# K1's scores by column halves and the WO result in halves, with a new order, in a chained attention kernel on one core

## The chip, the cores and the metric

The kernel runs on one core of a Trainium2 chip. The metric is the device time of one execution in microseconds, as the median of several runs.

## The reference

A pre-norm block: attention with a recurrent memory, then a normed MLP. Sizes: 2048 tokens of width 512, 32 heads of 128, a memory of 8 rows, segments of 32 tokens, so 64 segments one after the other; MLP width 1792.

```python
for s in range(n_seg):
    xs = x[:, s * seg_len:(s + 1) * seg_len, :].copy()
    h = jnp.concatenate([mem, xs], axis=1)
    q = jnp.einsum('btd,dhe->bhte', h, Wq)
...
    scores = jnp.einsum('bhqe,bhke->bhqk', q, k) * scale
    scores = jnp.where(mask[None, None], scores, -1000000000.0)
    p = _softmax(scores, axis=-1)
    o = jnp.einsum('bhqk,bhke->bhqe', p, v)
    o = jnp.einsum('bhte,hed->btd', o, Wo)
    mem = o[:, :M, :].copy()
    outs.append(o[:, M:, :])
```

The eight memory rows of a segment's result feed the next segment's projections. That is the recurrence: projections, scores, softmax, value product, WO, memory rows, next segment. With h = x + attention(layernorm(x)), the output is h + MLP(layernorm(layernorm(h))).

## The kernel before, in words

The kernel records every operation with what it reads and writes (class `Sched`), then orders each engine's queue itself. TensorE's order is written out by hand in `ORDERS` (L37), one list for each class of segment (number modulo 4). The other engines' operations are placed by a list scheduler (`schedule`) that takes their due times from `PLAN` (L43) and, for some, their engine from `HOME` (L100); operations without a due time go by rank into gaps. `wire` then sets the semaphore waits. Each queue runs in order. `PHASE` (L25) gives the place in TensorE's instruction stream, modulo 256, at which a segment should begin, which filler weight loads (L870) are put in to reach.

A segment packs 24 new tokens and the 8 memory rows as a stationary operand `hT` of 128x32 per chunk of 128 input features (four chunks); the last eight tokens of every segment (`hB`) are projected four segments at a time, a block ahead, as filler work. The heads are in two halves, r = 0 and 1. In a segment:

- Q0, Q1, K0, K1 (L872, and L605 where the loaded weights are kept): projections of one half of the heads, four units of four matmuls of 128x512 each, one unit per chunk, into a PSUM bank.
- Copies of these on ACT (`kq`, L890, L891), then 32x32 turns on DVE into `QT` and `KALL` (L913), and a copy of the memory queries into `ZC` on POOL (L927).
- SC0, SC1 (L1037): the scores of the memory queries, onto a bank prefilled with the mask (L1012). Then on DVE the negated maximum `nmc` (L1045), on ACT two exponentials with sums (L1054), on DVE a reciprocal (L1059) and a product by it and by `even` (L1062, `PC`, a scalar-tensor-tensor, STT below) for each of two column groups, and a turn (`PTC`, L1064).
- V0, V1: projections of the values (L872); copies to `VS`.
- PV0, PV1 (L1075, L1080): the value products of the memory queries, both into banks 0 and 1, copied to `OT` (ACT, L890). PVA (L1143): the same for the ordinary queries of the segment before.
- WO (L1171): eight units of 128x256 into one bank; a turn on DVE (`TT`, L1183) and adds of its two halves: `hT` (L1177, the memory rows of the next segment) and `opT` (L1177, the finished rows).
- SA (L1105): the scores of the ordinary queries, with a softmax of its own on DVE, ACT and POOL (`nma`, `SA`, `sma`, `rsa`, `PA`, `PTA`, `BD`: L1115 to L1132).
- F0, F1: the filler, eight units per segment of the block's last eight tokens: K for class 0, Q for class 1, V for class 2, and WO for class 3 (L1210), with their copies and turns (`KB`, `QTB`, `VSB`, `TTB`).

Layernorms and their statistics (`stt`, `agg`, L806, L807; `st2`, L1249) also run on DVE, and the MLP follows after the last segment.

Of the kernel before, what the change touches and what calls it, by code (L numbers as in the profile page):

```python
# [1689 lines left out]
```

## Time and profile before

| | |
|---|---|
| median of 3 runs | 807.39 us (806.82 to 807.42) |
| profiled execution, span | 805.9 us |
| mean granted TensorE clock | 0.993 |
| busy: PE, DVE, ACT, POOL | 775.0, 621.0, 527.1, 349.6 us |

The profiled execution's own time is the span; the page gives no other for it, and it lies 1.5 us below the median of the runs. On a timeline line the columns are the start, the duration, the engine, the line of the kernel, the operation, its output and inputs, the partitions x elements, how many were merged, and in brackets the engine's idle time before it with what ended it. PE rows are matmuls, PEld their weight loads. In the groups the last columns are busy time, mean ns of one and idle time before.

### The profile page before, as it was taken

To read this page: it belongs to the slowest core of one execution; us is meant where nothing else is said; L and a number is where in the kernel's file an instruction comes from. 1 tells how busy PE (TensorE), PEld (TensorE's weight loads), DVE (VectorE), ACT (ScalarE), POOL (GpSimd) and SP (SyncE) were. 2 spreads that over 40 slices of the span, in tenths; PEclk is the share of its full clock that TensorE was granted. 3 is DMA by queue.
4 is the path that set the end of the run, shared out by engine and by line. 5 is a ranking of instruction groups with operands and counts; after the bars stand their busy time and mean duration, and the time that the engine had idled before them with its cause. 6 is when DMAs were issued, how large, how long until landed. Compare 5 with 4: busy or idle time off the path is not lost.

```text
span 805.9 us, 43594 instructions
## 1 busy us (share of the span) xinstructions
PE 775.0 (96%) x19308; PEld 422.5 (52%) x18891; DVE 621.0 (77%) x2008; ACT 527.1 (65%) x1522; POOL 349.6 (43%) x886
## 2 busy tenths in 40 slices
PE   3788999999999999999999999999999999999998
PEld 1345555555555555555555555555555555544443
DVE  3268897989898989898989898989899887824211
ACT  2446777777777777777777777777676766643342
POOL 5023334545454545454545454545463535267200
PEclk9989999999999999999999999999999999999999
DMA  9950010111101010101010202020212131264200
GB/s 340 392 185 16 4 29 11 30 31 29 31 21 39 17 43 17 43 11 50 9 45 10 50 11 50 11 49 3 51 29 62 40 86 29 88 170 130 69 27 26
DMA packets 65449, 48.03 MB, mean 60 GB/s; under 512 B 29028, under 2 KB 61676, under 8 KB 65260
## 3 DMA queue, kind: packets, MB, share of 16 engines
q1 hardware_dynamic: 64928, 44.98, 19.0%
q8 instruction: 150, 2.46, 1.2%
q14 instruction: 39, 0.32, 0.1%
q10 hardware_dynamic: 332, 0.27, 0.1%
HBM read 31.08 MB, written 8.13 MB: 49 GB/s over the span
## 4 chain that ended last, share of the span: by engine, by line
PE 91%; DVE 3%; DMA 2%; SPq 2%; ACT 1%; issue 1%; POOL 0%
PE ps L872 43%; PE ps L1171 16%; PE ps L605 6%; PE quad L1579 6%; PE ps L1572 5%; PE ps L1210 4%; PE quad L1075 3%; DMA WQ<-in_A_Wq_dram 2%; SPq L775 2%; PE ps L1105 2%; PE quad L1037 2%; PE ps L1365 2%; PE quad L1143 1%; PE quad L1080 1%; DVE PC L1062 1%; ACT kq L890 1%
## 5 line engine op out<-in xcount | busy, mean ns | idle before, releaser
L872 PE MATMUL ps<-WQ,hT 128*32 128x512 bf16 x2048 | 157.4, 382 | 3.4 <-DVE hT L1177 3.3
L1171 PE MATMUL ps<-WO,OT 128*32 128x256 bf16 x4224 | 140.8, 275 | 1.0 <-ACT OT L890 1.0
L872 PE MATMUL ps<-WV,hT 128*32 128x512 bf16 x1780 | 138.7, 379 | 0.0
L891 ACT ACTIVATE kq<-ps 128x512 bf16<-128x512 f32 x146 | 87.2, 597 | 63.7 <-PE ps L872 63.4
L1126 POOL TENSOR_TENSOR PA<-SA,rsa 128x256 bf16<-128x256 f32 x64 | 39.9, 624 | 183.0 <-DVE rsa L1119 170.6
L890 ACT CAST kq<-ps 128x512 bf16<-128x512 f32 x160 | 93.4, 584 | 38.2 <-PE ps L872 38.2
L1171 PEld LDWEIGHTS ps<-WO,OT 128*32 128x32 bf16 x4224 | 96.2, 97 | 26.5 <-ACT OT L890 12.3
L1132 POOL COPY BD<-PTA 32x192 bf16<-32x192 bf16 x256 | 95.5, 373 | 16.6 <-DVE PTA L1128 0.8
L1062 DVE SCALAR_TENSOR_TENSOR PC<-EC,rsc,even 128x128 bf16<-128x128 f32 x256 | 94.5, 370 | 6.7
L872 PE MATMUL ps<-WK,hT 128*32 128x512 bf16 x1292 | 92.5, 379 | 0.0
L872 PEld LDWEIGHTS ps<-WQ,hT 128*32 128x32 bf16 x2048 | 57.0, 96 | 57.9 <-issue 18.7
L913 DVE STREAM_TRANSPOSE KALL<-kq 128x256 f32<-128x256 f32 x160 | 70.5, 440 | 20.8 <-ACT kq L890 18.6
L1054 ACT ACTIVATE EC<-quad,nmc 128x64 f32<-128x64 f32 x252 | 77.1, 311 | 5.9 <-DVE nmc L1045 0.2
L605 PE MATMUL ps<-WK,hT 128*32 128x512 bf16 x756 | 74.6, 379 | 0.0
L890 ACT CAST VS<-ps 128x512 bf16<-128x512 f32 x126 | 73.7, 585 | 0.7
L890 ACT CAST OT<-quad 128x128 bf16<-128x128 f32 (+1 forms) x205 | 66.3, 363 | 7.5 <-PE quad L1080 5.7
L913 DVE STREAM_TRANSPOSE QT<-kq 128x256 f32<-128x256 f32 x128 | 57.0, 445 | 15.5 <-ACT kq L891 14.1
L872 PEld LDWEIGHTS ps<-WV,hT 128*32 128x32 bf16 x1780 | 50.5, 96 | 34.2 <-issue 1.0
L1575 ACT ACTIVATE WQ<-ps,b1t 128x512 bf16<-128x512 f32 x42 | 28.9, 688 | 52.0 <-PE ps L1572 52.0
L872 PEld LDWEIGHTS ps<-WK,hT 128*32 128x32 bf16 x1292 | 36.4, 97 | 46.1 <-issue 20.1
L1117 ACT ACTIVATE SA<-SA 128x256 f32<-128x256 f32 x64 | 26.7, 417 | 49.4 <-DVE SA L1116 45.0
L1223 POOL TENSOR_TENSOR opT<-TTB,TTS 32x64 bf16<-32x64 f32 x128 | 40.3, 315 | 31.7 <-DVE opT L1177 22.5
(160 smaller groups left out, 1477.9 us busy)
## 6 DMA issues: line engine op xcount, KB each, us to landing
WV<-in_A_Wv_dram SPq DMA_DIRECT2D x4, 1024.0 KB, 10.3
WK<-in_A_Wk_dram SPq DMA_DIRECT2D x4, 1024.0 KB, 18.0
WQ<-in_A_Wq_dram SPq DMA_DIRECT2D x4, 1024.0 KB, 19.0
WO<-in_A_Wo_dram SPq DMA_DIRECT2D x16, 256.0 KB, 7.6
v_last<-VSB SPq DMA_DIRECT2D x60, 64.0 KB, 3.1
VBD<-v_last SPq DMA_DIRECT2D x60, 64.0 KB, 2.8
h_mid<-xr SPq DMA_DIRECT2D x16, 128.0 KB, 1.8
WQ<-h_mid SPq DMA_DIRECT2D x4, 512.0 KB, 4.4
```

What stands on the lines that cost most here:

```text
L605: return e.add_instruction(mybir.InstMatmult(name="I-%d" % (4000000 + _kept[0]), engine=mybir.EngineType.PE, start_tensor_calc=start, stop ...
L872: ins = e.matmul(o, l, m, start=(k == 0), stop=(k == DC - 1), tile_position=(0, 32 * j), skip_group_check=True)
L890: return {"act": (lambda e: e.copy(out, src), t_act(n, ps_)), "dve": (lambda e: e.tensor_copy(out, src), 0.155 + 1.0e-3 * n * fast)}
L891: return {"act": (lambda e: e.mul(out, src, scale_), t_act(n, ps_)), "dve": (lambda e: e.tensor_scalar(out, src, scale_, None, ALU.mult), ...
L913: S.op("dve", lambda e: e.transpose(out, src), reads=[("kq", i)], writes=[key], dur=t_dve(256) + 0.02)
L1054: return e.activation(EC[:, r, sl, :], o[:, sl, :], ACTF.Exp, bias=nmc[:, r, sl:sl + 1], accum_out=smc[:, r, sl:sl + 1])
L1062: S.op("dve", lambda e, sl=sl, xc=xc: e.scalar_tensor_tensor(PC[:, r, :, :, sl], xc, rsc[:, r, sl:sl + 1], ev, ALU.mult, ALU.mult), reads= ...
L1132: S.narrow(S.op("pool", lambda e, j=j, rows=rows: e.tensor_copy(BD[rows, par, :, j, :, :], PTA[rows, :, 0:NA, :]), reads=["PTA"], writes=[ ...
L1171: ins = e.matmul(ps[bank][32 * j:32 * j + 32, 0:256], lhs(slot(h)), wo_cols(h, b), start=(k == 0), stop=(k == 15), tile_position=(0, 32 * ...
L1223: return e.tensor_tensor(o[32 * q:32 * q + 32, c:c + 2], x, y, ALU.add)
L1572: ins = e.matmul(ps[bank][:, 0:SBT], W1[:, cc, fc * P:(fc + 1) * P], hnT_of(k)[:, cc, :], start=(cc == 0), stop=(cc == DC - 1))
L1579: S.op("pe", lambda e: e.matmul(quad[:, t, :], gT_of(k, fc)[:, t * P:(t + 1) * P], W2[:, fc, :], start=(fc == 0), stop=(fc == FC - 1)), re ...
```

## The change

- K1 is projected by column halves (`half_passes`): eight units of four 128x256 matmuls in the order `KSEQ`, the first half into bank 2 and the second into bank 0. Each half has its own copy (`kql`, `kq`) and turn (`KAl`, `KA`).
- SC1 becomes SC1 and SC2, eight matmuls each, in banks 2 and 3, each with a prefill of its own (64 columns) and a maximum of its own (`nmc`, `nmd`). SC0 goes to bank 1.
- For the first half of the heads (`NRM` = 1) the two reciprocals and two STT become one reciprocal of two columns, a small product with `even` (`rse`) and one 128x256 product into `PC`. The second half keeps its two STT.
- WO's bank is turned in two halves (`TT2`), and the memory rows are added per half: chunks 0 and 1 first (`hTl`), then 2 and 3 (`hTm`). A projection unit waits only for its chunk's half.
- New `ORDERS`, `PLAN`, `HOME` and `PHASE`; a planned operation is never placed ahead of one planned before it on its engine.
- `PVM` and `P3` are off, so the paths they guard aren't built. All of PSUM becomes one tensor, `banks`, and `b1n` shares the place of `oN`.

```diff
-PHASE = (0, 64, 128, 192)
+PHASE = (11, 75, 139, 203)
+TT2, SPL, KCOL, PVM, NRM, P3 = True, True, True, False, 1, False
+KSEQ = ((0, 0), (1, 0), (1, 1), (0, 1), (0, 2), (0, 3), (1, 3), (1, 2))
...
-BANK = dict(K0=7, K1=6, Q0=6, Q1=5, V0=7, V1=5, F0=4, F1=6, FB=4, SA=5, WO=7, SC0=3, SC1=2)
+BANK = dict(K0=7, K1=2, KX=0, Q0=6, Q1=5, V0=7, V1=5, F0=4, F1=6, FB=4, SA=5, WO=7, SC0=1, SC1=2, SC2=3, PV0=5)
...
-                i = bisect.bisect_right(ST, t)
+                i = max(bisect.bisect_right(ST, t), placed[eng] + 1 if fixed else 0)
...
+        def half_passes(lhs, reads, slot, W, key, r, banks):
+            for n, (h, cc) in enumerate(KSEQ):
...
+                        w = W[:, cc, r * 2048:(r + 1) * 2048].rearrange("p (a y b e) -> p y a b e", a=4, y=2, b=2)[:, h, :, :, 32 * j:32 * j + 32]
+                        o, l, m = ps[banks[h]][32 * j:32 * j + 32, 0:256], lhs(cc), w
...
+            if r == 1 and SPL and s > 0:
+                for h, (a, b) in enumerate((("kql", "KAl"), ("kq", "KA"))):
...
+                    S.either(copy2(half, v, 256), reads=[("ps", bh)], writes=[(a, r)])
...
+                if not whole:
+                    S.op("dve", lambda e, sl=sl, o=o: e.tensor_reduce(nmc[:, r, sl:sl + 1], o[:, sl, :], AX.X, ALU.max, negate=True), reads=[bkey], writes=[("nmd" if sl else "nmc", r)], dur=0.22)
...
+            if NRM >> r & 1:
+                S.op("dve", lambda e: e.reciprocal(rsc[:, r, :], smc[:, r, :]), reads=[("sa", r), ("smc", r)], writes=[("rsc", r)], dur=0.16)
...
+                f = lambda e: e.tensor_tensor(PC[r][:].rearrange("p k t a -> p k a t"), bass.AP(x.tensor, x.offset, [list(x.ap[0]), [0, 2], [64, 2], [1, 64]]),
+                                              bass.AP(w.tensor, w.offset, [list(w.ap[0]), [2, 2], [1, 2], [0, 64]]), ALU.mult)
...
+            for h, k_ in enumerate(("TTl", "TT") if TT2 else ("TT",)):
+                w, c = (2, slice(2 * h, 2 * h + 2)) if TT2 else (4, slice(0, 4))
...
+                    S.op("dve", lambda e, c=c: [halves_add(tt, q2, hT[64 * q2:64 * q2 + 64, sl, c, NA:SEG], slice(NA, SEG), c)(e) for q2 in range(2)][1],
+                         reads=[(k_, par)], writes=[(HK[h], sl)], dur=0.36 if TT2 else 0.4)
```

What this makes of the queues is seen at three places. First TensorE in a class 0 segment, from the last unit of K1 to the value products. Before (WK,hT is K1, WV the values, WK,hB the filler, KALL,ZC the scores, PTC,VS is PV0):

```order
L872 MATMUL ps<-WK,hT 32x512 x12
L1037 MATMUL quad<-KALL,ZC 32x64 x16
L872 MATMUL ps<-WV,hT 32x512 x4
L605 MATMUL ps<-WV,hT 32x512 x4
L872 MATMUL ps<-WV,hT 32x512 x12
L872 MATMUL ps<-WK,hB 32x512 x4
L1037 MATMUL quad<-KALL,ZC 32x64 x16
L872 MATMUL ps<-WV,hT 32x512 x4
L872 MATMUL ps<-WK,hB 32x512 x4
L872 MATMUL ps<-WV,hT 32x512 x8
L872 MATMUL ps<-WK,hB 32x512 x4
L1075 MATMUL quad<-PTC,VS 128x2x16 x8
```

The same stretch of TensorE's queue in the changed kernel (L631 keeps the loaded weights):

```order
L925 MATMUL banks<-WK,hT 32x256 x4
L1099 MATMUL banks<-KALL,ZC 32x64 x16
L905 MATMUL banks<-WV,hT 32x512 x4
...
L631 MATMUL banks<-WV,hT 32x512 x4
L1099 MATMUL banks<-KALL,ZC 32x64 x8
L905 MATMUL banks<-WV,hT 32x512 x4
L631 MATMUL banks<-WV,hT 32x512 x4
L1099 MATMUL banks<-KALL,ZC 32x64 x8
L905 MATMUL banks<-WV,hT 32x512 x4
L631 MATMUL banks<-WV,hT 32x512 x4
L905 MATMUL banks<-WK,hB 32x512 x12
L1208 MATMUL banks<-PTC,VS 128x2x16 x8
```

Six units stood between SC0 and SC1 and five between SC1 and PV0; now four stand before the first part, two between the parts and five behind the second.

Second, DVE in the same stretch, from the second turn of QT to the second PTC. Before:

```order
L913 STREAM_TRANSPOSE QT<-kq 128x256
L1045 TENSOR_REDUCE nmc<-quad 128x2
L913 STREAM_TRANSPOSE KALL<-kq 128x256
L1059 RECIPROCAL rsc<-smc 128x1
L1062 SCALAR_TENSOR_TENSOR PC<-EC,rsc,even 128x128
L1059 RECIPROCAL rsc<-smc 128x1
L1045 TENSOR_REDUCE nmc<-quad 128x2
L1062 SCALAR_TENSOR_TENSOR PC<-EC,rsc,even 128x128
L1064 STREAM_TRANSPOSE PTC<-PC 128x128
L1059 RECIPROCAL rsc<-smc 128x1
L1062 SCALAR_TENSOR_TENSOR PC<-EC,rsc,even 128x128
```

DVE's queue at that place in the changed kernel (rse and the 128x2x2x64 product are the first half's, the two maxima 128x1 the second's):

```order
L965 STREAM_TRANSPOSE QT<-kq 128x256
L1110 TENSOR_REDUCE nmc<-banks 128x2
L979 STREAM_TRANSPOSE KALL<-kq 128x4x32 x2
L1116 TENSOR_REDUCE nmc<-banks 128x1
L1137 RECIPROCAL rsc<-smc 128x2
L1139 TENSOR_TENSOR rse<-rsc,even 128x4
L1142 TENSOR_TENSOR PC<-EC,rse 128x2x2x64
L1116 TENSOR_REDUCE nmc<-banks 128x1
L1148 RECIPROCAL rsc<-smc 128x1
L1153 STREAM_TRANSPOSE PTC<-PC 128x128
L1151 SCALAR_TENSOR_TENSOR PC<-EC,rsc,even 128x128
```

The second part's maximum and the first reciprocal of the second half now stand ahead of the first PTC.

Third, DVE at the end of a class 2 segment, from the second PTC to the scores of SA. In the changed kernel (stt and st are statistics of the layernorms, agg their aggregates):

```order
L1153 STREAM_TRANSPOSE PTC<-PC 128x128
L942 CAST OT<-banks 128x16x24
L1317 TENSOR_TENSOR opT<-TT 64x4x24 x2
L1073 COPY banks<-maskCF 128x64
L836 BN_STATS stt<-xr 128x6
L837 BN_AGGR agg<-stt 128x2
L1392 BN_STATS st<-xr 128x6
L1325 STREAM_TRANSPOSE TT<-banks 128x128
L1396 BN_AGGR agg<-st 128x2
L1317 TENSOR_TENSOR hT<-TT 64x2x8 x2
L1325 STREAM_TRANSPOSE TT<-banks 128x128
L1255 TENSOR_REDUCE nma<-banks 128x8
```

Before, two OT casts, a 128-column mask copy, stt and agg stood between PTC and the single TT, and st stood elsewhere. In class 0 the two opT adds stand behind rsa and ahead of the first QT in the changed kernel:

```order
L1357 STREAM_TRANSPOSE TTB<-banks 128x512
L1258 TENSOR_REDUCE sma<-SA 128x8
L1259 RECIPROCAL rsa<-sma 128x8
L1317 TENSOR_TENSOR opT<-TT 64x4x24 x2
L965 STREAM_TRANSPOSE QT<-kq 128x256
```

Before, that place had TTB, sma, rsa and QT alone, and the opT adds stood behind the second PTC.

More of the change, by code (lines that the diff above doesn't have):

```diff
@@ L1027, in sc_mm @@
             reg = 2 + bk % 2
+            heads = range(4) if part is None else range(2 * part, 2 * part + 2)
             def f(e):
-                for i in range(4):
+                for i in heads:
                     for j in range(4):
@@ new lines, in pair, with late_rows @@
+        def pair(s, r):
+            return 0 if r == 0 or not P3 else BANK["PV1"] if s > 0 else 2
+        def late_rows(s, r):
+            bk, sg = s // 4, s % 4
+            b0 = pair(s, r)
+            src = bass.AP(banks[:].tensor, banks[:].offset + 512 * b0 + MEM, [list(banks[:].ap[0]), [512, 2], [16, 8], [1, 8]])
+            ot = OTB[:, bk % 2, :, 8 * sg:8 * sg + 8].rearrange("p (t r k) q -> p r t k q", t=2, r=2)[:, r]
+            S.either(copy2(ot, src, 128), reads=[("ps", b0), ("ps", b0 + 1)], writes=[("OTB" if r else "OTC", bk % 2, sg)])
@@ L1081, in f @@
+                    ins = e.matmul(o, VBD[rows, bk % 2, sg, r, :], PTC[r][rows, :, 32:64, :].rearrange("p b q a -> p b a q"),
                                    start=False, stop=True, tile_position=(64 * t, 0), skip_group_check=True)
                 return ins
-            S.op("pe", f, reads=[("VS", s % 3, r), ("PTC", r)] + [("VBD", bk % 2, j) for j in range(4)], writes=CQ, dur=0.205, mode=MH, ni=20)
-            src = bass.AP(quad[:].tensor, quad[:].offset + 128 * r, [list(quad[:].ap[0]), [512, 2], [16, 8], [1, MEM]])
+            S.op("pe", f, reads=[("VS", s % 3, r), ("PTC", r)] + [("VBD", bk % 2, j) for j in range(4)], writes=both, dur=0.205, mode=MH, ni=20)
```

399 lines of the change are left out of this document (264 added, 135 removed), and 6 rows, old and new, of the table ORDERS.

## Prediction

> **What bounds the kernel now.** The page first, for its span; then the timeline of one segment on all engines; then the busy time by segment; then the groups by form, for prices.
>
> ```profile
> span 805.9 us, 43594 instructions
> ```
>
> A PE that the views call busy can hide waits, since the ends of matmuls are modelled; their starts tell more. Here is the segment that begins at 411.86 (class 0, by number modulo 4); the last row is the fourth next start of Q0.
>
> ```profile
> 411.86 0.41 PE L872 MATMUL ps<-WQ,hT 128*32 128x512 bf16 x4
> 415.32 0.30 PE L1037 MATMUL quad<-KALL,ZC 128*32 128x64 bf16 x16
> 416.74 0.30 PE L1037 MATMUL quad<-KALL,ZC 128*32 128x64 bf16 x16
> 416.87 0.40 PE L872 MATMUL ps<-WV,hT 128*32 128x512 bf16 x4
> 418.07 0.27 PE L1075 MATMUL quad<-PTC,VS 64*128 64x32 bf16 x8
> 418.54 0.40 PE L872 MATMUL ps<-WK,hB 128*32 128x512 bf16 x4
> 418.83 0.62 PE L1171 MATMUL ps<-WO,OT 128*32 128x256 bf16 x16
> 419.38 0.27 PE L1075 MATMUL quad<-PTC,VS 64*128 64x32 bf16 x8
> 419.64 1.50 PE L1171 MATMUL ps<-WO,OT 128*32 128x256 bf16 x48
> 420.96 0.39 PE L872 MATMUL ps<-WK,hB 128*32 128x512 bf16 x4
> 421.18 0.42 PE L1105 MATMUL ps<-KALL,QT 128*32 128x32 bf16 x32
> 421.43 0.84 PE L872 MATMUL ps<-WK,hB 128*32 128x512 bf16 x12
> 422.14 0.40 PE L872 MATMUL ps<-WQ,hT 128*32 128x512 bf16 x4
> ...
> 453.00 0.43 PE L872 MATMUL ps<-WQ,hT 128*32 128x512 bf16 x4
> ```
>
> Four segments take 453.00 - 411.86 = 41.14 us. Sixteen 512-column units fill 411.86 to 415.32, so a unit costs 0.216. From 416.87 five units should end at 417.95; PV0 (L1075) starts at 418.07, a wait of 0.12. The unit at 418.54 ends at 418.75, WO at 418.83: 0.08. WO's two units cost 2 x 0.22 (six take 1.32 from 419.64), so PV1 could start at 419.27 and starts at 419.38: 0.11. From 420.96 come four units and SA (421.18 to 421.43): 422.07 against 422.14, 0.07. Together 0.38 per segment: all that a shorter chain can win, some 23 us in the 62 segments after the first two. What ends these waits stands on DVE and ACT:
>
> ```profile
> 414.23 0.45 DVE L913 STREAM_TRANSPOSE QT<-kq 128x256 f32<-128x256 f32 x1 [0.37 <-ACT kq L891]
> 414.71 0.45 DVE L913 STREAM_TRANSPOSE KALL<-kq 128x256 f32<-128x256 f32 x1
> 415.31 0.45 DVE L913 STREAM_TRANSPOSE QT<-kq 128x256 f32<-128x256 f32 x1
> 415.71 0.29 DVE L1045 TENSOR_REDUCE nmc<-quad 128x2 f32<-128x128 f32 x1
> ...
> 416.34 0.31 ACT L1054 ACTIVATE EC<-quad,nmc 128x64 f32<-128x64 f32 x1
> 416.54 0.20 ACT L1054 ACTIVATION_READ_ACCUMULATOR EC<-quad,nmc 128x1 f32 x1
> 416.53 0.12 DVE L1059 RECIPROCAL rsc<-smc 128x1 f32<-128x1 f32 x1
> 417.70 0.31 DVE L1064 STREAM_TRANSPOSE PTC<-PC 128x128 f32<-128x128 f32 x1
> 418.49 0.67 ACT L890 CAST OT<-quad 128x128 bf16<-128x128 f32 x2
> 418.96 0.31 DVE L1064 STREAM_TRANSPOSE PTC<-PC 128x128 f32<-128x128 f32 x1
> 421.19 0.45 DVE L1183 STREAM_TRANSPOSE TT<-ps 128x256 f32<-128x256 f32 x1 [0.29 <-PE ps L1171]
> 421.67 0.39 DVE L1177 TENSOR_TENSOR hT<-TT 64x32 bf16<-64x32 f32 x2
> ```
>
> PV0 follows the first PTC by 0.37, PV1 the second by 0.42, Q0 the end of hT by 0.08: DVE ends three of the four waits. And DVE has little room. Of the four classes, the segment with the least DVE time and the one with the most (the third number of busy time, after PE and PEld):
>
> ```profile
> 411.86:422.14 10.28, 10.28 (x297) 5.75 (x283) 9.00 (x32) 7.41 (x22) 5.04 (x13) 1.00 0.04 10
> 432.42:442.70 10.28, 10.28 (x296) 5.78 (x280) 9.62 (x33) 7.42 (x22) 5.66 (x15) 1.00 0.01 3
> ```
>
> The order of work is therefore a chain through one in-order DVE queue, with TensorE filled around it.
>
> **The change, step by step.** I walk one segment of the new order; times count from the start of Q0, whose row above is 0. Prices come from these groups:
>
> ```profile
> L1062 DVE SCALAR_TENSOR_TENSOR PC<-EC,rsc,even 128x128 bf16<-128x128 f32 x256 | 94.5, 370 | 6.7
> L1177 DVE TENSOR_TENSOR opT<-TT 64x96 bf16<-64x96 f32 x128 | 33.8, 264 | 3.0
> L1116 DVE TENSOR_TENSOR SA<-ps,nma 128x256 f32<-128x256 f32 x64 | 27.1, 424 | 2.2
> L1177 DVE TENSOR_TENSOR hT<-TT 64x32 bf16<-64x32 f32 x126 | 24.7, 196 | 3.0
> ```
>
> *K1 and the scores.* K1's sixteen matmuls of 512 columns become 32 of 256. At WO's 0.11 for four of those K1 costs 0.88 instead of 0.864. The first half is done at 3.25 and the second at 3.47. A reader of PSUM follows PE by 0.23 (TT, 421.19, after 420.96), so ACT's copies begin at 3.48 and 3.75, with the 64-column mask copy behind them at 4.02, still ahead of the first exponential at 4.18 (nmc's end, 4.14, and a hop). DVE turns the halves behind nmc at 4.05 and 4.28, at 0.31 each like PTC. The first part of SC1 can run at 4.46, where TensorE gets to it, the second at 4.96; before, SC1 ran at 4.88. Splitting it I cost at nothing, since its matmuls are the same and stand between V units; bounds 0 and 0.13, another SC slot (416.74 to 416.87). The new banks (0 for K1's second half, 1 for SC0) are those of PV0 and PV1, which come long after the last read there. Three more filler loads ahead of Q0 I cost at nothing, at most 0.06 (PEld, 5.75 us for 283 loads).
>
> *First half of the heads.* The second exponential starts at 4.49 (4.48 before); its sum is read about 0.4 later. Then DVE does one reciprocal at 4.92, a four-column product at 5.08 (priced as a reciprocal, 0.12 to 0.15, plus 0.03 to the next), and one 128x256 product at 5.26 in place of two STT. No row shows that product. The nearest by kind and size is L1116, 0.424; the upper bound scales L1062, whose output it shares (two-byte elements, every other one): hT and opT give (264 - 196)/64 = 1.06 ns a column and 0.16 fixed, so L1062 has (370 - 160)/128 = 1.64 ns a column, and 256 columns take 0.58. I take 0.424. Independent DVE instructions follow 0.06 before the end of the last one (415.31 to 415.71 is 0.40 for a 0.45), so the second part's maximum starts at 5.62, and a reciprocal at 5.76. Both stand between the product and PTC0, which starts at 5.87 (5.84 before), so PV0 at 6.24 (6.21 before): nothing gained here.
>
> *Second half.* The last exponential waits for that maximum, and on ACT for the copy of V0: 5.96. PTC0, STT (0.24 later), reciprocal (6.40), STT (6.58), PTC1 at 6.98 instead of 7.10. So PV1 could start at 7.40. TensorE: PV0 is at 6.24. Its OT copy came 0.42 later, behind V1's copy on ACT; now it is ahead of that, and where ACT was free it took 0.37:
>
> ```profile
> 398.83 0.27 PE L1075 MATMUL quad<-PTC,VS 64*128 64x32 bf16 x8
> 399.20 0.27 ACT L890 CAST OT<-quad 128x128 bf16<-128x128 f32 x1 [0.18 <-PE quad L1080]
> ```
>
> So the copy is at 6.61, WO 0.34 behind it (418.49 to 418.83) at 6.95, and PV1 at 7.39 to 7.40 (7.52 before). WO ends at 8.98 (9.10).
>
> *The WO result in halves.* TT's first half starts 0.23 after WO's end as before, the add of two chunks follows 0.32 later, and two adds of 64x16 take 0.36 (between 2 x 0.16 and 2 x 0.196), so Q0 can start 0.97 after WO's end. TensorE has four units and SA there, 1.11. So the wait of 0.07 goes, and the next Q0 is at 8.98 + 1.11 = 10.09. The second half (turn, then nma, then its adds) is ready 1.90 after WO's end; K0's third unit, the first that reads chunk 2, comes at 1.11 + 0.86 = 1.97.
>
> *What DVE pays.* Classes 1 and 3 have their other work (0.24 from PTC1, then OT casts, opT, copies) done by 2.12 to 2.24 after PTC1, where TT can start at 2.23. Class 2 doesn't: its tail held stt and agg and ran into TT already,
>
> ```profile
> 439.55 0.31 DVE L1064 STREAM_TRANSPOSE PTC<-PC 128x128 f32<-128x128 f32 x1
> 439.79 0.98 DVE L890 CAST OT<-quad 128x384 bf16<-128x384 f32 x2
> ...
> 441.00 0.68 DVE L806 BATCH_NORM_STATS2 stt<-xr 128x6 f32<-128x512 bf16 x1
> 441.72 0.18 DVE L807 BATCH_NORM_AGGREGATE agg<-stt 128x2 f32<-128x6 f32 x1
> 441.82 0.42 DVE L1183 STREAM_TRANSPOSE TT<-ps 128x256 f32<-128x256 f32 x1
> ```
>
> 2.27 from PTC1 to TT, where 2.23 is needed (418.96 to 421.19). In the new order one OT cast (0.49) gives way to two opT adds (2 x 0.264 less an overlap, about the same), a mask copy loses 64 of its columns (0.07), and a 256-column statistic joins (stt's 0.68 less 256 columns, 0.41, less the overlap 0.36): 2.56, so 0.33 late. Less the slack of 0.14, plus a small aggregate between TT and its add (0.05), Q0 comes 0.24 later: 10.33. Chunk 2 of hT is then some 0.09 late in class 3: 10.18.
>
> In class 0 two opT adds (0.5) now stand ahead of QT. SA's steps begin 0.26 later there, behind the second turn and the second pair of adds; the queue had 0.37 idle before QT (414.23). So QT comes 0.5 + 0.26 - 0.37, less an overlap, 0.33 late. KALL, 0.48 behind QT because it waited for ACT, can follow by 0.37; SC0 comes about 0.2 late, and the segment takes 10.29. Where opT stood before, behind PTC1, it was covered by WO's units; ahead of QT nothing covers it.
>
> *Sum.* 10.29 + 10.09 + 10.33 + 10.18 = 40.89 against 41.14: 0.25 per four segments, 15 times 3.8 us. In the first three segments, which have no filling units behind WO, PV1 comes 0.12 earlier and Q0 another 0.16 (WO's end to Q0 1.18 before, 1.02 with chunk 2): 3 x 0.28 = 0.8. Start and feed-forward stage keep their instructions but for small ones. Together -4.6. The profiled execution spans 805.9 us; the median of the runs, 807.39, lies 1.5 above it and the page gives no other time of that execution, so I leave 1.5 as it is: 807.39 - 4.6 = 802.8 us.
>
> **The rivals.**
> *The tails fit.* If stt, agg and opT find gaps (DVE has 0.7 to 1.3 idle per segment above) and all classes run at 10.09, it is 40.36, so 15 x 0.78 + 0.8 = 12.5 less: 794.9 us. Against it: the rows from 439.55 to 441.82 leave no gap.
> *The added DVE work eats it.* If adds of 64x16 cost as much as 64x32 (0.196), each pair takes 0.42, chunk 2 comes 0.12 later than above and its slack of 0.07 turns into a wait of 0.05 in every class; with a little more at the turned halves, 0.07 per segment: 4.4 us, about 807, no change. For it: 196 and 264 show that most of such an instruction is fixed.
> *The wide product is slow.* If the 128x256 product takes 0.58 as L1062's slope gives, PTC0 comes at 6.03, and PV0, both later PTC and PV1 all 0.16 later: 63 x 0.16 = 10.1, so 807.39 - 4.6 + 10.1 = 812.9 us, slower. It decides from 4.6 / 63 = 0.07 lost per segment, a product of 0.50. For it: L1062 is 0.08 longer than an equal tensor-tensor step. [...]
>
> **How the numbers follow.** The walk 0.45 (802.8, own range 798 to 806: 0.07 either way per segment), the tails fit 0.20, no change 0.15, the slow product 0.20. About 0.2% (1.6 us) is what a measurement of this kernel can tell from no change. Faster: 0.40 of the walk and 0.20, 0.60. Within: 0.04 and 0.13, 0.17. Slower: 0.20 and the rest, 0.23. The range reaches from 794 to 811.5, leaving out the ends of the first and the last case.
>
> **What would show it.** Right: PTC0 near 5.87 and PTC1 near 6.98 after Q0; PV1 near 7.40; classes 1 and 3 shorter than 0 and 2; TT of class 2 behind stt. The product's mean tells the third rival (0.42 or 0.58). Wrong: Q0 waiting for hT in class 1, SC1's parts waiting for their copies, or an unchanged PTC1.

## The result, and the profile after

The changed kernel takes 834.15 us (median of 4 runs, 833.30 to 834.26), the kernel before 807.4: a ratio of 1.0328 with a 95% interval of 1.0313 to 1.0343. It is slower by 26.7 us where 4.6 us less had been forecast. The profiled executions span 805.9 and 831.6 us, so 25.7 us lie in the trace. One run of a kernel below, `e6_b_wide`, took 894.88 us at a granted clock of 0.849 and is left out of its median.

The page of the changed kernel, its first line:

```profile
span 831.6 us, 43972 instructions
```

TensorE's timeline, a class 0 segment and the start of the class 1 segment behind it (L905 and L631 are projections, L1099 scores, L1208 value products, L1311 WO):

```profile
426.06 0.47 PE L905 MATMUL banks<-WQ,hT 128*32 128x512 bf16 x4
426.30 0.44 PE L631 MATMUL banks<-WK,hT 128*32 128x512 bf16 x4
...
427.00 0.40 PE L905 MATMUL banks<-WK,hT 128*32 128x512 bf16 x4
...
430.37 0.30 PE L1099 MATMUL banks<-KALL,ZC 128*32 128x64 bf16 x16 [0.59 <-POOL ZC L988]
...
433.25 0.27 PE L1208 MATMUL banks<-PTC,VS 64*128 64x32 bf16 x8
...
433.94 0.62 PE L1311 MATMUL banks<-WO,OT 128*32 128x256 bf16 x16
434.49 0.27 PE L1208 MATMUL banks<-PTC,VS 64*128 64x32 bf16 x8
...
436.07 0.60 PE L905 MATMUL banks<-WK,hB 128*32 128x512 bf16 x8
...
437.30 0.40 PE L905 MATMUL banks<-WQ,hT 128*32 128x512 bf16 x4
437.63 0.38 PE L631 MATMUL banks<-WK,hT 128*32 128x512 bf16 x4
...
438.06 0.38 PE L631 MATMUL banks<-WQ,hT 128*32 128x512 bf16 x4
438.32 0.40 PE L905 MATMUL banks<-WK,hT 128*32 128x512 bf16 x4
```

Units stand 0.216 apart, so K0 should start 0.22 behind Q0 and the fifth unit 0.87. In class 1 they come at 0.33 (437.63) and 1.02 (438.32). In class 0, SC0 comes at 4.31 instead of 3.46. From SC0 on less has changed in class 0: PV0 follows by 2.88 (before 2.75), PV1 by 4.12 (4.06), and from WO's end (436.07) to Q0 it is 1.23 (1.18). In classes 1 to 3 SC0 comes 0.17, 0.35 and 0.15 later than before (medians), and the eighth unit 0.16, 0.34 and 0.15 later, so there SC0 pays for the units ahead of it. Class 3 also shows that the forecast gain at Q0 is real: Q0 follows WO's end by 1.10 there (median; 1.17 before, 1.11 forecast), and SC0 gives it back.

The busy time by segment, from Q0 to Q0, for classes 0, 1, 2 and 3:

```profile
426.06:437.30 11.24, 10.57 (x312) 5.20 (x266) 10.53 (x37) 7.32 (x24) 4.81 (x11) 1.00 0.02 4
437.30:447.71 10.41, 10.41 (x313) 5.19 (x270) 9.61 (x35) 7.78 (x25) 3.68 (x11) 1.00 0.01 4
447.71:458.60 10.89, 10.62 (x314) 5.24 (x272) 10.13 (x38) 8.20 (x26) 6.96 (x19) 1.00 0.01 4
458.60:468.90 10.30, 10.30 (x308) 5.23 (x274) 9.46 (x35) 7.03 (x23) 4.75 (x13) 1.00 0.37 98
```

Four segments take 42.84 us instead of 41.14; 15 times the difference of 1.70 is 25.5 us, nearly all of the 25.7. No class is shorter than before. DVE's busy time, the third number of the engines, is up to 9.5 to 10.5 from 9.0 to 9.6.

What DVE and POOL do at the start of that class 0 segment:

```profile
426.17 0.39 DVE L1255 TENSOR_REDUCE nma<-banks 128x8 f32<-128x256 f32 x1
...
426.59 0.36 DVE L1317 TENSOR_TENSOR hT<-TT 64x16 bf16<-64x16 f32 x2
...
426.98 0.42 DVE L1256 TENSOR_TENSOR SA<-banks,nma 128x256 f32<-128x256 f32 x1
...
428.36 0.20 DVE L1259 RECIPROCAL rsa<-sma 128x8 f32<-128x8 f32 x1
...
428.60 0.85 DVE L1317 TENSOR_TENSOR opT<-TT 64x96 bf16<-64x96 f32 x2
428.65 0.69 POOL L1266 TENSOR_TENSOR PA<-SA,rsa 128x256 bf16<-128x256 f32 x1 [5.00 <-DVE rsa L1259]
...
429.46 0.45 DVE L965 STREAM_TRANSPOSE QT<-kq 128x256 f32<-128x256 f32 x1
...
429.97 0.29 POOL L988 COPY ZC<-QT 128x128 bf16<-128x128 bf16 x1 [0.64 <-DVE QT L965]
```

SA's add (L1256) is at Q0 + 0.92, behind the second turn and the second pair of hT adds. In the segment of class 3 before, with Q0 at 401.59, nma began before Q0 and the add came at + 0.42:

```profile
401.55 0.42 DVE L1115 TENSOR_REDUCE nma<-ps 128x8 f32<-128x256 f32 x1
...
402.01 0.43 DVE L1116 TENSOR_TENSOR SA<-ps,nma 128x256 f32<-128x256 f32 x1
```

Then come the opT adds, and they take 0.85. QT, which ZC and so SC0 wait for, is at Q0 + 3.40 (2.37 before). The end of the class 2 segment on DVE (WO ends at 457.12):

```profile
456.59 0.69 DVE L836 BATCH_NORM_STATS2 stt<-xr 128x6 f32<-128x512 bf16 x1
457.32 0.18 DVE L837 BATCH_NORM_AGGREGATE agg<-stt 128x2 f32<-128x6 f32 x1
457.42 0.39 DVE L1392 BATCH_NORM_STATS2 st<-xr 128x6 f32<-128x256 bf16 x1
457.73 0.30 DVE L1325 STREAM_TRANSPOSE TT<-banks 128x128 f32<-128x128 f32 x1
457.95 0.17 DVE L1396 BATCH_NORM_AGGREGATE agg<-st 128x2 f32<-128x12 f32 x1
458.15 0.36 DVE L1317 TENSOR_TENSOR hT<-TT 64x16 bf16<-64x16 f32 x2
```

TT starts 0.61 after WO's end where 0.23 would do: 0.38 late. The groups of the disputed prices:

```profile
L1317 DVE TENSOR_TENSOR hT<-TT 64x16 bf16<-64x16 f32 x252 | 50.1, 199 | 5.8
L1317 DVE TENSOR_TENSOR opT<-TT 64x96 bf16<-64x96 f32 x128 | 39.6, 309 | 2.9
L1142 DVE TENSOR_TENSOR PC<-EC,rse 128x256 bf16<-128x256 f32 x64 | 30.2, 472 | 2.5 <-POOL rse L1139 0.3
```

The adds of 16 columns have the same mean as those of 32 (199 against 196 ns), and there are twice as many. The means include pairs beside POOL's adds and copies, most of which take longer (see the last section): where POOL is idle, a pair takes 0.36 against 0.39.

### The profile page after: what moved, and what is told of

Read it like the earlier page. It is cut to its first block, busy times and chain, and to the rows that moved or that the text cites. A ratio compares the mean times of both kernels' runs of the same rounds, so it can differ in the third digit from the quotient of the medians.

```text
span 831.6 us, 43972 instructions
## 1 busy us (share of the span) xinstructions
PE 785.3 (94%) x20320; PEld 393.6 (47%) x17843; DVE 663.6 (80%) x2289; ACT 533.4 (64%) x1619; POOL 350.7 (42%) x887
## 4 chain that ended last, share of the span: by engine, by line
PE 65%; DVE 26%; SPq 5%; issue 2%; DMA 1%; POOL 1%; ACT 0%
PE banks L905 18%; PE banks L631 13%; PE banks L1311 11%; PE banks L1745 6%; PE banks L1738 4%; DVE hT L1317 3%; DVE opT L1317 3%; PE banks L925 3%; DVE PC L1142 2%; DVE TT L1325 2%; PE banks L1208 2%; SPq L822 2%; SPq L805 2%; PE banks L1099 2%; PE banks L1353 2%
## 5 line engine op out<-in xcount | busy, mean ns | idle before, releaser
L1311 PE MATMUL banks<-WO,OT 128*32 128x256 bf16 x4224 | 140.7, 275 | 0.7 <-ACT OT L942 0.5
L905 PE MATMUL banks<-WQ,hT 128*32 128x512 bf16 x1292 | 106.3, 381 | 5.0 <-DVE hT L1317 4.8
L943 ACT ACTIVATE kq<-banks 128x512 bf16<-128x512 f32 x146 | 87.2, 597 | 33.3 <-PE banks L905 30.8
L631 PE MATMUL banks<-WK,hT 128*32 128x512 bf16 x1512 | 107.8, 308 | 0.0
L1311 PEld LDWEIGHTS banks<-WO,OT 128*32 128x32 bf16 x4224 | 96.4, 97 | 22.2 <-issue 2.2
L942 ACT CAST kq<-banks 128x256 bf16<-128x256 f32 (+1 forms) x209 | 89.0, 457 | 24.0 <-PE banks L905 20.4
L631 PE MATMUL banks<-WV,hT 128*32 128x512 bf16 x1024 | 101.2, 378 | 0.0
L905 PE MATMUL banks<-WV,hT 128*32 128x512 bf16 x1024 | 101.2, 378 | 0.0
L1119 ACT ACTIVATE EC<-banks,nmc 128x64 f32<-128x64 f32 x256 | 79.5, 313 | 18.5 <-DVE nmc L1110 9.6
L1257 ACT ACTIVATE SA<-SA 128x256 f32<-128x256 f32 x64 | 26.7, 417 | 90.6 <-DVE SA L1256 90.6
L942 ACT CAST VS<-banks 128x512 bf16<-128x512 f32 x126 | 74.2, 589 | 2.3
L631 PE MATMUL banks<-WQ,hT 128*32 128x512 bf16 x756 | 75.4, 379 | 0.0
L942 ACT CAST OT<-banks 128x128 bf16<-128x128 f32 (+1 forms) x176 | 56.1, 328 | 26.1 <-PE banks L1213 20.1
L1099 PEld LDWEIGHTS banks<-KALL,ZC 128*32 128x32 bf16 x2048 | 39.1, 96 | 61.0 <-DVE KALL L979 30.7
L905 PEld LDWEIGHTS banks<-WQ,hT 128*32 128x32 bf16 x1292 | 36.3, 96 | 53.3 <-issue 31.7
L1099 PE MATMUL banks<-KALL,ZC 128*32 128x64 bf16 x2048 | 49.8, 194 | 9.3 <-POOL ZC L988 8.0
## 6 DMA issues: line engine op xcount, KB each, us to landing
WV<-in_A_Wv_dram SPq DMA_DIRECT2D x4, 1024.0 KB, 10.5
```

What stands on the lines that cost most here:

```text
L631: return e.add_instruction(mybir.InstMatmult(name="I-%d" % (4000000 + _kept[0]), engine=mybir.EngineType.PE, start_tensor_calc=start, stop ...
L905: ins = e.matmul(o, l, m, start=(k == 0), stop=(k == DC - 1), tile_position=(0, 32 * j), skip_group_check=True)
L942: return {"act": (lambda e: e.copy(out, src), t_act(n, ps_)), "dve": (lambda e: e.tensor_copy(out, src), 0.155 + 1.0e-3 * n * fast)}
L943: return {"act": (lambda e: e.mul(out, src, scale_), t_act(n, ps_)), "dve": (lambda e: e.tensor_scalar(out, src, scale_, None, ALU.mult), ...
L1099: ins = e.matmul(o[32 * j:32 * j + 32, sl, :], ZC[:, par, h, :], rhs, start=False, stop=(i == heads[-1]), tile_position=(0, 32 * j), skip_ ...
L1119: return e.activation(EC[:, r, sl, :], o[:, sl, :], ACTF.Exp, bias=nmc[:, r, sl:sl + 1], accum_out=smc[:, r, sl:sl + 1])
```

## The experiments

Thirteen more kernels ran. The table gives medians, the ratio to the kernel before with its 95% interval, and for the middle blocks of each profiled execution the median period of classes 0, 1, 2, 3 (Q0 to Q0), all in us. The runs of before beside them had medians of 807.7 to 808.8.

| kernel | median | ratio | class 0 | 1 | 2 | 3 | sum |
|---|---|---|---|---|---|---|---|
| before | 807.4 | 1 | 10.28 | 10.33 | 10.27 | 10.27 | 41.2 |
| changed | 834.15 | 1.0313 to 1.0343 | 11.23 | 10.41 | 10.89 | 10.31 | 42.8 |
| e1_opT | 830.95 | 1.0268 to 1.0311 | 10.98 | 10.41 | 10.90 | 10.36 | 42.7 |
| e2_whole | 821.94 | 1.0166 to 1.0199 | 10.75 | 10.48 | 10.31 | 10.28 | 41.8 |
| e3_bank | 841.57 | 1.0403 to 1.0436 | 11.23 | 10.56 | 11.04 | 10.48 | 43.3 |
| e4_nrm | 834.43 | 1.0318 to 1.0349 | 11.22 | 10.41 | 10.89 | 10.36 | 42.9 |
| e5_b_halves | 832.28 | 1.0267 to 1.0310 | 10.70 | 11.07 | 10.63 | 10.67 | 43.1 |
| e6_b_wide | 814.77 | 1.0048 to 1.0092 | 10.31 | 10.34 | 10.40 | 10.39 | 41.4 |
| e7_clean | 823.57 | 1.0155 to 1.0205 | 10.56 | 10.86 | 10.30 | 10.40 | 42.1 |
| e8_late_k0 | 838.08 | 1.0338 to 1.0387 | 10.38 | 11.05 | 10.58 | 10.79 | 42.8 |
| e9_clean2 | 817.26 | 1.0097 to 1.0127 | 10.56 | 10.34 | 10.30 | 10.28 | 41.5 |
| e10_clean_stt | 818.68 | 1.0113 to 1.0157 | 10.77 | 10.34 | 10.31 | 10.25 | 41.7 |
| e11_b_bank | 831.71 | 1.0277 to 1.0308 | 10.70 | 10.75 | 10.62 | 10.66 | 42.7 |
| e12_b_freed | 830.35 | 1.0252 to 1.0295 | 10.72 | 10.73 | 10.66 | 10.72 | 42.8 |
| e13_pv1_late | 837.84 | 1.0343 to 1.0390 | 11.11 | 10.72 | 10.70 | 10.70 | 43.2 |

**First, one part undone at a time.** The theory after reading the trace: DVE's queue at the segment's two ends makes the loss, by the halves of WO's result and by opT ahead of QT. The rivals were PSUM banks and the wide product.

The opT adds of class 2 go behind the second PTC of the next class 0:

```diff
-        "opA": (19.034, 17.684, 22.988, 17.945),
+        "opA": (19.034, 17.684, 28.2, 17.945),
```

> One number of the plan changes: in class 0 the two opT adds that stood ahead of the first QT stand behind the second PTC, beside the pair that is there already. Theory (the adds ahead of QT are what makes class 0 long, 11.24 us, but its tail has no room for a second pair): SC0 comes at about 3.6 us after Q0 instead of 4.31, TT comes 0.4 to 0.5 late, class 0 takes 10.9, so 15 x 0.3 = 4 to 6 us less: about 829 us. Rival (the tail absorbs the pair): class 0 at 10.45, 15 x 0.8 = 12 us less: 822. Rival (class 0 is late for PA and ZC on POOL, not for opT): SC0 stays above 4.1 and the time at 834.

Measured: 830.95. SC0 of class 0 comes at 3.52 instead of 4.31, and from WO's end to Q0 it is 1.77 instead of 1.23: 0.79 won in front, 0.54 lost at the end. The theory held in both halves: the adds ahead of QT cost what the trace shows, and the one other place tried, behind the second PTC, isn't free either.

WO's result turned and added whole:

```diff
-TT2, SPL, KCOL, PVM, NRM, P3 = True, True, True, False, 1, False
+TT2, SPL, KCOL, PVM, NRM, P3 = False, True, True, False, 1, False
-        "TT": (10.017, 9.826, 9.826, 9.586),
+        "TT": (9.41, 9.219, 9.219, 9.219),
-        "hTm": (10.587, 10.396, 10.396, 10.396),
+        "hTm": (9.997, 9.806, 9.806, 9.566),
```

> The result of WO is turned and added whole, as before (TT2 off, TT and hT due where the first halves were; with less on DVE, the statistic st also leaves the end of class 2). Theory (the halves lose: they cost DVE some 0.6 us a segment, K0 waits for the second turn and its third unit for the second adds): class 0 11.24 to 11.0, class 1 10.41 to 10.3, class 2 10.89 to 10.5, class 3 10.30 unchanged, 15 x 0.75 = 11 us less: about 823. Rival (the halves win, the rest loses): Q0 comes some 0.1 later in each segment without them, 62 x 0.1 = 6 us more: 840.

Measured: 821.94, 12 us less; the theory's 823. K0 follows Q0 by 0.23 and the fifth unit by 0.87 in every class, and classes 2 and 3 are back at 10.31 and 10.28. The halves were to make the kernel faster and are the largest part of the loss. The run changes a second thing, though: the statistic st leaves the end of class 2 and goes to the start of class 1, which doesn't get shorter (10.48). In class 2 SC0 gains 0.34 and the way from WO's end to Q0 0.23 (1.24 instead of 1.47); the second is the place that st left, so some 15 x 0.23 = 3.5 of the 12 us can't be told from st's move. Class 0 is still 10.75: SC0 is at 3.82 there, with the opT adds still ahead of QT.

K0 out of the bank that WO's result is turned from:

```diff
-BANK = dict(K0=7, K1=2, ...
+BANK = dict(K0=2, K1=7, ...
```

> K0 and K1's first half exchange their banks (K0 in 2, K1's first half in 7), so that K0 no longer writes the bank that WO's result is turned from; the rest is as in the changed kernel. Theory (K0's wait for the second turn, 0.02 to 0.1 a segment, lies under the wait of its third unit for the second adds, which DVE's queue sets): K0 follows Q0 by 0.22, its third unit starts where it did, and the time stays within 1 us of 834. Rival (the bank is a cause of its own): 62 x 0.1 = 6 us less: 828.

Measured: 841.57, outside both. K0 does follow by 0.23, and the fifth unit starts where it did (1.20 in class 2, 1.01 in class 3), as the theory said. But K1's first half now sits in V0's bank, so V0 waits for its copy: in classes 1 to 3 it is 1.08 from SC0 to SC1 instead of 0.98, and PV0 comes 0.16 later (2.93 after SC0 instead of 2.77). The exchange took away one wait and made another; the bank had to be asked again, below.

The wide product out, by `NRM` = 0 and the due times of the kernel before for its four steps:

> The first half of the heads gets its two reciprocals and two STT back (NRM = 0, due as before); the wide 128x256 product (0.47) and the small product rse are gone. Theory (the product isn't the cause): PTC0 stays within 0.05 of 2.42 after SC0, and the time within 3 us of 834. Rival (the wide product and rse, 0.16 to 0.32, cost the chain): PV0 comes 0.1 to 0.16 earlier, 62 x 0.1 = 6 to 10 us less: 824 to 828.

Measured: 834.43, no change. PV0 comes 2.73 after SC0 instead of 2.77, but PV1 and the period stay where they were (4.00 after SC0; 10.40 and 10.89 in classes 1 and 2). The product isn't the cause.

**Second, one part alone in the kernel before.** All of its tables stay. The halves alone, with due times for the new steps:

```diff
+TT2, SPL, KCOL, PVM, NRM, P3 = True, False, False, False, 0, False
-        "TT": (9.37,) * 4,
+        "TTl": (9.37,) * 4,
+        "hTl": (9.77,) * 4,
+        "TT": (9.8,) * 4,
-        "hTm": (9.86,) * 4,
+        "hTm": (10.35,) * 4,
```

> The order, due times and banks of the kernel before, K1 and SC1 whole, two STT per half; of the change only the turn and the adds of WO's result in two halves (second half between the first adds and nma, second adds behind nma, as in the changed kernel). Theory (two adds of 64x16 cost as much as two of 64x32, so Q0 gains at most its 0.07, and K0 waits for the second turn and its third unit for the second adds): 0.05 to 0.15 more per segment, 62 times, 810 to 816 us. Rival (the halves do gain at Q0 what was forecast, the loss is elsewhere): 0.07 less, 62 times, 803.

Measured: 832.28, far over either. The halves alone cost 24 us. Three waits show: K0 0.25 to 0.33 after Q0, the fifth unit 0.95 to 1.03, and Q1, whose bank 5 also holds SA's scores: SA's add now comes later, so Q1's first unit, the sixth, waits and the eighth starts 1.85 to 1.93 after Q0 instead of 1.52. SC0 follows at 3.81 to 4.17. Class 1 (11.07) has a fourth: on POOL two copies that wait for a DMA stand ahead of PA and ZC there, and its segments scatter from 10.51 to 11.35.

K0 moved to bank 1, which nothing uses at that time (`K0=1` in `BANK`; the clean form of the question that the exchange had spoilt):

> The kernel before with the result of WO in halves, and K0 in bank 1 (free at that time) instead of bank 7, which WO's result is turned from. Theory (K0's wait for the second turn lies under the later waits, of Q0's third unit for the second adds and of Q1 for bank 5, which SA's add reads): K0 follows Q0 by 0.22, the units behind start where they did, and the time stays at 831 to 833. Rival (the bank has a price of its own): 0.05 to 0.1 less a segment, 826 to 829.

Measured: 831.71. K0 follows by 0.23, the fifth unit still by 0.95 to 1.03, and nothing is won. The wait for the bank is real and hidden: the wait behind it ends at the same moment with or without it. Class 1's other median (10.75 against 11.07) is its scatter, 10.54 to 11.52 here.

Then all three waits taken away:

```diff
-BANK = dict(K0=1, K1=6, Q0=6, Q1=5, ...
+BANK = dict(K0=1, K1=6, Q0=6, Q1=0, ...
-        "nma": (10.17,) * 4,
+        "nma": (10.4,) * 4,
-        "hTm": (10.35,) * 4,
+        "hTm": (10.1,) * 4,
```

> The kernel before with the result of WO in halves and all three waits behind it taken away by other banks and another order: K0 in bank 1 and Q1 in bank 0 (not 5, which SA's scores use), and the second adds of hT ahead of nma instead of behind it. Theory (those waits are the whole price of the halves, and Q0 gains its 0.07): 10.2 to 10.3 a segment, 803 to 809 us. Rival (the four more DVE instructions of each segment push SA's steps and so QT and SC0 back): SC0 later than 3.55, 815 us or more.

Measured: 830.35. The theory fell and the rival stood. The first units run without a wait (0.22, 0.87, 1.52), and SC0 is still late, at 3.70 to 3.79. DVE, POOL and TensorE there, in a class 3 segment with Q0 at 412.88:

```profile
413.19 0.36 DVE L1306 TENSOR_TENSOR hT<-TT 64x16 bf16<-64x16 f32 x2
413.57 0.42 DVE L1244 TENSOR_REDUCE nma<-banks 128x8 f32<-128x256 f32 x1
414.03 0.42 DVE L1245 TENSOR_TENSOR SA<-banks,nma 128x256 f32<-128x256 f32 x1
...
415.39 0.20 DVE L1248 RECIPROCAL rsa<-sma 128x8 f32<-128x8 f32 x1
415.51 0.40 DVE L954 STREAM_TRANSPOSE QT<-kq 128x256 f32<-128x256 f32 x1
...
415.67 0.62 POOL L1255 TENSOR_TENSOR PA<-SA,rsa 128x256 bf16<-128x256 f32 x1 [3.08 <-DVE rsa L1248]
...
416.23 0.29 POOL L977 COPY ZC<-QT 128x128 bf16<-128x128 bf16 x1
...
416.57 0.31 PE L1088 MATMUL banks<-KALL,ZC 128*32 128x64 bf16 x16
```

In the kernel before, with Q0 at 411.86, POOL had time between PA and ZC:

```profile
413.94 0.62 POOL L1126 TENSOR_TENSOR PA<-SA,rsa 128x256 bf16<-128x256 f32 x1 [4.25 <-DVE rsa L1119]
...
414.75 0.29 POOL L927 COPY ZC<-QT 128x128 bf16<-128x128 bf16 x1 [0.18 <-DVE QT L913]
```

From SA's add to rsa it takes 1.36 (1.38 before), with an exponential on ACT between. The add is at Q0 + 1.15 instead of 0.42, and rsa ends at 2.71 instead of 2.0. QT, behind rsa on DVE, loses less, 0.26 (2.63 instead of 2.37), since DVE had 0.37 idle ahead of it. What SC0 waits for is ZC, and the wait is on POOL: PA needs rsa, stands ahead of ZC in POOL's queue and ends at 3.41, and ZC follows without a gap, 0.32 behind QT's end, where it took 0.07 before. So ZC is 0.46 late (3.35 instead of 2.89); the 0.28 that lay between its end and SC0 absorb a part, and SC0 pays the rest. The rival named QT; the chain that it fits is SA, rsa, PA, ZC. Two limits: the second adds ahead of nma put SA's add 0.15 later than in the run before (1.16 instead of 1.01 in classes 0 and 2), and no run placed ZC ahead of PA, so it isn't shown that the halves must cost this. Here PV0 also comes 2.91 after SC0 instead of 2.74; why isn't settled.

The wide product alone in the kernel before (`NRM` = 1, the small product due at 5.2):

> The kernel before with one part of the change alone: for the first half of the heads one reciprocal, the small product rse and one 128x256 product in place of two reciprocals and two STT. Theory (a wash, as the run that took this part out said): PTC0 within 0.05 of 2.38 after SC0, 805.5 to 809. Rival (in the old order the three steps stand later than the STT that ran beside the second exponential): PV0 0.08 later, 62 x 0.08 = 5 us more: 812.

Measured: 814.77, some 6 us more: the rival's time. PV0 comes 2.83 after SC0 instead of 2.74. A likely reason, not tested: in the old order the first STT ran while the second exponential did, and one product for both has to wait for both sums. But PV1 comes only 0.03 later, and classes 0 and 1 lose no more than that. Classes 2 and 3 lose 0.12 to 0.13, because ACT's queue there also has a mask copy ahead of the second half's copy of OT, which WO waits for (at Q0 + 8.02 instead of 7.88 in class 2). So about half of the 6 us comes from a copy that moved with the product and not from the product. In the new order PV0 comes 0.04 later with it, and this lies under other waits.

**Third, what is left without the halves.** From the kernel with WO's result whole, the queue is cleared: opT of class 2 as above, the turn KB1 behind SA's add, and the copy kq5 on ACT:

```diff
-        "KB1": (9.032, None, None, None),
+        "KB1": (10.95, None, None, None),
-'kq5': 'dve'
+'kq5': 'act'
```

> The changed kernel with WO's result turned and added whole, and DVE's queue cleared at three places: class 2's opT adds go from ahead of QT to behind the second PTC of class 0, the copy kq5 of the filler goes from DVE to ACT, and the turn KB1 of class 0 stands behind SA's add. K1 by halves, the scores in two parts and the wide product stay. Theory (the loss is all in the DVE queue at the segment's two ends): classes at 10.3, 10.3, 10.3, 10.29, 41.2 for four, so 804 to 809 us. Rival (the split itself loses too, since PV1 waits for the copy of VS that now stands behind the OT copy on ACT): classes at 10.4 to 10.5, 812 to 816.

Measured: 823.57, worse than both. Class 0 came down to 10.56, but class 1 rose to 10.86: there kq5 stands on ACT ahead of the copy of OT that WO waits for, and the turn of kq5 at the head of DVE's queue waits for ACT. With kq5 on ACT in class 0 alone and QTB1 due at 10.95:

> Second attempt at the cleared DVE queue, with WO's result whole: class 2's opT adds behind the second PTC of class 0, kq5 on ACT in class 0 alone (in class 1 it had stood ahead of the copy of OT that WO waits for), the turns KB1 and QTB1 behind SA's add. K1 by halves and the wide product stay. Theory (what is left of the loss beside the halves is the DVE queue at the segment's ends): classes 0 to 3 at 10.40, 10.32, 10.31, 10.29, so 41.3 for four and 808 to 813 us. Rival (other DVE or ACT work slips in the way again): 818 to 824.

Measured: 817.26, between theory and rival. Classes 1, 2 and 3 are at 10.34, 10.30 and 10.28, so with the halves gone the queue was all that was wrong there. Two things stay open: class 0 (10.56, where SC1 comes 0.12, PV0 0.15 and PV1 0.27 later after Q0 than in class 3, and from WO's end on nothing more is lost) and the first segment after the opening, which takes 13.1 us (Q0 at 51.71 and 64.79) against 10.3 before.

The same with two STT for the first half (`NRM` = 0), so that only the split of K1 and SC1 and the order are left:

> As the run before it in this list, with two reciprocals and two STT for the first half of the heads in place of the wide product. What is left of the change is K1 by halves, SC1 in two parts and the new order. Theory (PV1 never waited for the second PTC: it starts 0.55 after WO's first two units whatever PTC does, so the split can win only what PV0 and the OT copy behind it win, 0.05 a segment): PV1 at 7.46 after Q0, 804 to 809 us, within 3 us of the kernel before. Rival (the forecast's chain: PV1 follows the second PTC, 0.12 earlier): 799 to 803.

Measured: 818.68, above both, by class 0 (10.77) and the first segment (12.9). In class 3, where nothing is in the way, TensorE shows what the split is worth:

```profile
449.68 0.41 PE L905 MATMUL banks<-WQ,hT 128*32 128x512 bf16 x4
...
455.88 0.27 PE L1208 MATMUL banks<-PTC,VS 64*128 64x32 bf16 x8
...
456.60 0.61 PE L1311 MATMUL banks<-WO,OT 128*32 128x256 bf16 x16
457.14 0.27 PE L1208 MATMUL banks<-PTC,VS 64*128 64x32 bf16 x8
...
459.92 0.50 PE L905 MATMUL banks<-WQ,hT 128*32 128x512 bf16 x4
```

PV1 is at 7.46 instead of 7.51, as the theory has it, and the segment takes 10.24 instead of 10.27. No version found here beats the kernel before: some 0.03 in class 3 is all that the split brings, classes 1 and 2 gain nothing (10.34 and 10.31), and class 0 loses.

An attempt to keep the halves, with opT, kq5 and KB1 as in the first clearing:

```diff
-('Q0', 0, 1), ('K0', 0, 2), ('Q0', 1, 2), ('K0', 2, 3),
+('Q0', 0, 2), ('K0', 0, 3),
-        "nma": (10.245, 10.054, 10.054, 10.054),
+        "nma": (10.6, 10.41, 10.41, 10.41),
-        "hTm": (10.587, 10.396, 10.396, 10.396),
+        "hTm": (10.24, 10.05, 10.05, 10.05),
```

> As the kernel with the cleared queue (opT, kq5 and KB1 moved), but WO's result in halves, with nma behind the second adds instead of ahead of them, and TensorE's order begins with two units of Q0 and then K0, so that K0 comes 0.43 after Q0 and not 0.22. Theory (then nothing waits for the second turn or the second adds, and Q0 comes 0.1 earlier than with the whole turn): 10.15 to 10.25 a segment, 798 to 803 us. Rival (the four more DVE instructions of a segment, some 0.55 us, make another step late): no better than the whole turn, 806 to 812.

Measured: 838.08. K0's waits are gone, and SC0 is at 3.66 to 3.80 in classes 1 to 3, 0.05 behind ZC's end: the same price by the same chain as in the freed kernel, plus class 1's misplaced kq5. In class 0 SA's add comes at 0.78 in the median, SC0 isn't late (3.46), and the segment takes 10.38.

**Fourth, did PV1 ever wait for PTC?** The last run places PV1 behind four units of WO (`('WO', 0, 4), ('PV1', 0, 99), ('WO', 4, 8)` in the kernel before):

> The kernel before with one change of TensorE's order: PV1 stands behind four units of WO instead of two, so that the second PTC is done some 0.5 us before TensorE comes to PV1. Theory (the 0.11 between the end of WO's units, by 0.22 each, and PV1 is not a wait for PTC but comes with the change from WO to PV1): four units and PV1 0.99 apart, 4 x 0.22 + 0.11; the segment grows, since WO's second half now waits for the copy of OT, 0.3 a segment, 825 us. Rival (it is a wait for PTC, as the prediction read it): 0.88 apart.

WO, PTC on DVE, and PV1 in that run:

```profile
425.06 1.06 PE L1171 MATMUL ps<-WO,OT 128*32 128x256 bf16 x32
425.19 0.31 DVE L1064 STREAM_TRANSPOSE PTC<-PC 128x128 f32<-128x128 f32 x1
...
426.05 0.27 PE L1075 MATMUL quad<-PTC,VS 64*128 64x32 bf16 x8
```

And in the kernel before with the wide product:

```profile
422.94 0.62 PE L1299 MATMUL banks<-WO,OT 128*32 128x256 bf16 x16
...
422.98 0.31 DVE L1141 STREAM_TRANSPOSE PTC<-PC 128x128 f32<-128x128 f32 x1
...
423.49 0.27 PE L1196 MATMUL banks<-PTC,VS 64*128 64x32 bf16 x8
```

Measured: PTC is done 0.55 before PV1, and PV1 still comes 0.99 after WO's start, so in all 62 segments behind the opening. Behind two units it comes after 0.55, with PTC done 0.11 (before), 0.20 (with the wide product, the second view) or up to 0.34 earlier (with opT moved). The 0.11 beyond the units is a fixed cost of going from WO to PV1. The time, 837.84, is more than the 825 expected: beside WO's second half, which waits for OT as said, class 0 lost 0.43 at PV0, where the turn TTB (0.67) had moved on DVE from behind SA's add to ahead of nmc.

## Why the prediction was wrong, by its steps

*What bounds the kernel.* "DVE ends three of the four waits" was misread. The wait at PV1 is no wait, so a shorter softmax of the second half can't win it. PV0's 0.12 is mostly of the same kind: with the product undone, PTC0 ends 0.10 to 0.11 ahead of PV0 instead of 0.06, and three filler units and PV0 stand 0.76 apart, 3 x 0.216 + 0.11; before, one unit and PV0 stood 0.34 apart, some 0.02 more than 0.216 + 0.11. Of the 0.38 per segment some 0.15 could be won, at WO and at Q0. The sentence "DVE has little room" was right, and should have outweighed the rest.

*Splitting K1 and the scores.* Right in its durations: in class 3 PTC0 led to PV0 2.77 after SC0 (forecast 2.78). The step to PV1 failed: the forecast has WO's two units end at PV0 + 1.15, the trace has PV1 at PV0 + 1.24 in every class, because of the 0.11. Forecast gain at PV1 0.12, there was 0.02 to 0.05 in classes 2 and 3 once the halves were gone.

*The wide product.* Forecast 0.424 between bounds of 0.424 and 0.58, measured 0.472, below the 0.50 from which the third rival was to decide. So its condition didn't come about: undoing the product changed nothing in the new order (834.43), and in the cleared order it made the kernel 1.4 us slower (817.26 to 818.68). That it cost 6 us alone in the old order, near the 5.5 of that rival, is luck: PV1 came 0.03 later there and not 0.16, and about half of the loss came by the mask copy. The measured 0.472 is nearer to L1116's 0.424 than to the 0.58 estimated from L1062's slope.

*The WO result in halves.* This is the step that failed most, by three omissions; the gain at Q0 that it was made for did come where the end of the segment was free (class 3). K0's bank was not looked at; that cost nothing by itself. The second half was forecast ready 1.90 after WO's end, 0.07 before K0's third unit needs it. With both pairs of adds at 0.36 it was ready at 1.98 and TensorE started 0.06 behind that (class 0); beside POOL's adds and copies a pair took 0.43 to 0.54 (classes 1 and 2). So the unit was late by 0.07 to 0.33. And SA's steps were taken to be 0.26 later in class 0 only, with 0.37 idle to absorb it; they came 0.5 to 0.75 later in every class, and behind them stand QT and, on POOL, PA and ZC: in class 0 that is the loss, and with the other waits taken away it is what is left. The halves cost 12 us in the new order, some 3.5 of them not to be told from st's move, and 24 in the old. The second rival had this mechanism (the added DVE work eats the gain), and far too small a price for it, 4.4 us.

*Class 0.* Right mechanism, wrong size: QT was forecast 0.33 late and came 1.03 late. SA's steps took 0.50 instead of 0.26, and the opT adds 0.85 instead of 0.5, where they run beside PA on POOL. KALL was named as what SC0 waits for; it was ZC, behind QT.

*Class 2.* Right: TT 0.38 late where 0.33 was forecast; from WO's end to Q0 it is 1.48 instead of 1.18. That is the end of the segment; class 2's other loss, 0.35 at SC0, is that of the halves.

*The sum.* Undone one behind the other, the halves (with st's move) take away 12.2 us (834.15 to 821.94), and the opT adds, kq5, KB1 and QTB1 4.7 (to 817.26). The kernel before took 807.84 beside that run, so 9.4 are left: class 0 has 15 x 0.28 = 4.2, the first segment 2.8 (in the changed kernel it takes 11.5, so part of this came with the undoing), and 2.4 are spread. Why these are lost stays open.

## What to carry to other kernels

Before a gap on a timeline is booked as a wait, see whether it shrinks where the producer is done earlier: 0.54 to 0.56 between the same two instructions in nearly every segment, whether the producer is done 0.11 or 0.34 earlier, is a cost and not a slack. When a step on a queue with a tenth of its time free is split in two, price what stands behind it up to the next engine's use (here SA, rsa, PA on POOL, ZC, SC0), not only the step that was to come earlier. A wait that is found and removed may be worth nothing when a second one ends at the same moment; take it away alone, with nothing else moved, before it is called a cause. And look at what did move: in two runs here (the wide product alone, PV1 behind four units) a step that nobody had named changed its place and made a part of the difference.
